# Moving the return of x ahead of the powers' row, the loads and the stores in SyncE's queue of a gated linear attention and cosine MLP kernel

## The chip, the cores and the metric

The kernel runs on one core of one Trainium2 chip. The metric is the device time of one execution in microseconds (us), as the median of several runs. The profile is of one further execution, whose own time is given beside its span (from its first to its last recorded instruction).

## What is computed

An attention-like recurrence, then an MLP with a cosine gate. Cut to what matters:

```python
# q, k, v, a_re, a_im: (B, H, S, D) = (4, 8, 768, 48)
mag = sqrt(a_re**2 + a_im**2)
scale = minimum(mag, 0.999) / (mag + 1e-6)
ar, ai = a_re * scale, a_im * scale              # a complex decay per step and channel
for t in range(S):
    S_re, S_im = ar*S_re - ai*S_im + k[t] (x) v[t], ar*S_im + ai*S_re
    y[t] = q[t] @ S_re
x = y.transpose(0, 2, 1, 3).reshape(3072, 384)
h = x @ w_in                                     # 384 -> 2048
out = (h * cos(h)) @ w_out                       # 2048 -> 384
```

## The kernel before, in words

The sequence is cut into 24 chunks of 128 steps, six to a batch. Two chunks make a group g, of which there are 12 (0 to 11). A group passes through these steps, and each step of it is a function of `fast_path`:

- `load`: re, im, k, q, v of the group come from memory by DMAs on SyncE's queue.
- `log_steps` (`logs`): the logarithm of the decay's size and the tangent of its half angle. ScalarE squares re and im (`lg<-re`, `tan<-im`), loads a table, takes `lg`, `mag`, `rs`; VectorE does `lg<-lg,tan`, `mag<-re,mag`, `lg<-lg`, `lg<-lg,rs`, `mag<-mag,tan`, `lo<-lg,hi`, `tan<-...`, in turn with ScalarE.
- `p_powers`, `g_carry`, `g_split`, `even_steps`, `p_apply` (`prods`): TensorE sums the logarithms along the chunk (`lgs`), ScalarE exponentiates them into P (kept in the buffer of `lg`) and Q, VectorE rounds them and multiplies k and q by them (`Q<-k,Q`, `mag<-q,lg`).
- `row_out`, `row_back`: the last row of P goes to memory as `row` (one packet of 3072 bytes) and comes back transposed as `end` (96 partitions x 16 elements; two DMAs of 768 elements of 4 bytes each). `p_end` halves `end` and keeps its least value. `state_next` reads `end`.
- `g_phase`, `g_trig`, `g_stack` (`phases`, `keys`): the angles are summed (`phs`), their sine and cosine taken, and `ks` and `qs` formed. `f_transpose` turns them by way of memory: a block transpose on VectorE (`tr`), a DMA to memory (`moved`), and DMAs back as `kT` (four) and `qT` (one). All of these are on SyncE's queue.
- `chunks`: for each chunk two `f_scores` (TensorE's `sc`, masked by VectorE into the halves of `atm`: four heads each), `f_state` (`sp`, then `state` on VectorE), and `f_out` (`yp`: eight heads in pairs, each atm half read by two pairs; where a chunk has a state, its product with q is added). ScalarE copies `yp` into `yT`. After the group's second chunk `f_x` writes yT to memory as `x` (two DMAs), and `f_xt` reads it back, laid out for the MLP, as `xT`.
- `mm1_sums`, `gate_sine`, `gate_product` (`first`): `hp` = w_in times xT on TensorE, in eight parts of 12 matmuls; ScalarE takes the cosine (`gate`) and a square sum (`junk`), VectorE the product.
- `mixed`, `seventh` (`mixes`, `products`): from group 2 on the second product is done by a seven-product scheme. VectorE forms sums and differences of gates (`s`); TensorE's `sum` and `op` accumulate; ScalarE and VectorE write `ot`; a store on SyncE's queue writes it out. Groups 0 and 1 use `mm2`, with its own store.

The main loop runs over n from 2 to 11. An iteration begins with the scores of group n, and beside them stand the logs of group n+1 and the second product of group n-1; then come the keys of n+1 and, from 0.56 of the iteration on, the first product of group n. `weave` sets the order in which the instructions are written down, by the fractions beside each part. In TensorE's queue this order is binding, since `matmul` chains each instruction to the one before. On VectorE, ScalarE and SyncE the order in this loop is left to the scheduler, which places instructions by its own estimate of when they can run; `behind(a, b)` keeps a behind b in a queue, without a wait of its own.

Every vector and scalar operation is recorded at the helper's lines L676 (`Ordered`) and L707 (`special`), and matmuls at L687, so they are told apart by their tiles. The DMAs concerned are recorded at these lines: L581 and L584 loads, L835 `row`, L842 `end`, L933 `moved`, L936 `kT`, L938 `qT`, L1048 `x`, L1057 `xT`, L1113, L1196 and L1202 stores.

In SyncE's queue of a steady iteration the order is: re and im of group n+2 (ten DMAs), `row`, `x` twice, `end` twice, `k`, `xT`, `k`, `q` twice, `v` twice, two stores, `moved` twice, `kT` four times, `qT`.

Of the kernel before, what the change touches and what calls it, by code (L numbers as in the profile page):

```python
# [487 lines left out]
def fast_path(ctx, tc, q, k, v, a_re, a_im, moe_w_in, moe_w_out, out, least, odd, wide,  # L488
# [7 lines left out]
    nc = tc.nc  # L496
    B, H, S, D = q.shape
    DM, DF = moe_w_in.shape
    C = 128
    NCH = S // C  # L500
    G = 2
    N = B * NCH
    NG = N // G
# [30 lines left out]
    late = {}  # L534
# [8 lines left out]
    def behind(ins, other):  # L543
        tc.add_manual_dep(ins.ins, other.ins.name, mybir.DependencyInfo(
            mybir.DependencyClass.NoSync, mybir.DependencyReason.DATA))
# [14 lines left out]
    X = [dict() for _ in range(NG)]  # L560
# [6 lines left out]
    def load(g, names, i=None, put=nc.sync.dma_start):  # L567
        for name in names:
            ap = {"re": a_re, "im": a_im, "q": q, "k": k, "v": v}[name]
            if name not in X[g]:  # L570
                X[g][name] = ld.tile([C, G, H, D], F32, tag=name, name=name,
                                     bufs=2 if name == "v" else 1)
            b, c = divmod(g * G + (i or 0), NCH)
            one, n = i or 0, G if i is None else 1
            steps = ap[b].rearrange("h (c p) d -> p c h d", p=C)[:, ds(c, n)]
            tile_ = X[g][name][:, ds(one, n)]
            parts = [(0, C, 0)]
            if name in ("re", "im") and g >= PEG:

                parts = [(0, C - 16, 1), (C - 16, C - 1, 1)]  # L580
                put(out=tile_[C - 1:C], in_=steps[0:1])  # L581
            for i_ in range(n):
                for lo, hi, by in parts:
                    put(out=tile_[lo:hi, i_], in_=steps[lo + by:hi + by, i_])  # L584
# [227 lines left out]
    def even_steps(g, i, n):  # L812


        x = X[g]
        u = cut(x["mag"], i, n)
        P, Q = cut(x["P"], i, n), cut(x["Q"], i, n)
        ins = [vector.scalar_tensor_tensor(out=u, in0=Q, scalar=HUGE, in1=P,
                                           op0=ALU.min, op1=ALU.mult)]
        yield  # L820
        for t in P, Q:
            ins.append(vector.scalar_tensor_tensor(out=t, in0=u, scalar=3.0, in1=t,
                                                   op0=ALU.subtract, op1=ALU.mult))
            yield

        for one_, what in zip(ins, ("carried", "split")):
            if what in x and g > PEG:
                behind(one_, x[what])
        if g > 0:
            row_out(g, i, n, nc.sync)  # L830
            row_back(g, i, n, nc.sync)

    def row_out(g, i, n, queue):
        P = cut(X[g]["P"], i, n)
        queue.dma_start(out=X[g]["row"][ds(i * DM, n * DM)],  # L835
                        in_=P[C - 1:C].rearrange("o x -> (o x)"))

    def row_back(g, i, n, queue):
        row = X[g]["row"][ds(i * DM, n * DM)]
        end = X[g]["end"][:, ds(i * H, n * H)]  # L840
        for a in range(2):
            queue.dma_start(out=end[ds(a * D, D)], in_=row.rearrange("(x d) -> d x", d=D))  # L842
# [209 lines left out]
    def f_xt(g, i=0, n=G):  # L1052

        if i == 0:
            X[g]["xT"] = msb.tile([C, ND, G, C], F32, tag="xT", name="xT")
        moved = X[g]["moved"].rearrange("p s d g t -> (p s d) g t").rearrange("(c r) g t -> r c g t", r=C)
        put = nc.sync.dma_start(out=X[g]["xT"][:, :, ds(i, n)], in_=moved[:, :, ds(i, n)])  # L1057
        behind(put, late["x"])
        late["x"] = put

    def mm1_sums(g, jp, i=None):

# [39 lines left out]
    def mm2(g, i, j0, nj):  # L1102
        if j0 == 0:
            Y[g * G + i]["op"] = pm.tile([C, DM], F32, tag="acc" if g == i else "m", name="op",
                                         bufs=1 if g == i else 2)
        ps = Y[g * G + i]["op"]
        for j in range(j0, j0 + nj):
            matmul(ps, lhsT=X[g]["gate"][j // 2][:, j % 2, ts(i, C)], rhs=w_out[:, j],
                   start=(j == 0), stop=(j == NJ - 1))
        if j0 + nj == NJ:  # L1110
            ot = msb.tile([C, DM], F32, tag="ot", name="ot")
            scalar.mul(out=ot, in_=ps, mul=1.0 / (in_scale * out_scale))
            nc.sync.dma_start(out=out[ts(g * G + i, C), :], in_=ot)  # L1113

# [1 line left out]
    PLAIN, HJ, E2 = 2, NJ // 2, DM // 2  # L1118
# [41 lines left out]
    def seventh(g, p, part):  # L1160


        x, name = X[g], SEVEN[p]
        if p == 0 and part == 0:
            x["sum"] = pm.tile([C, E2], F32, tag="acc", name="sum", bufs=1)
            x["ot"] = [msb.tile([C, DM], F32, tag="ot", name="ot") for _ in range(G)]

        alone = g == NG - 1 and p == 6
        summed = p in (0, 3, 5, 6) and not alone
        if not summed and part == 0:  # L1170
            x["op"] = pm.tile([C, E2], F32, tag="m", name="op", bufs=2)
        ps = x["sum"] if summed else x["op"]
        for j in range(part * HJ // 2, (part + 1) * HJ // 2):
            matmul(ps, lhsT=left(g, name, j), rhs=right[name][:, j],
                   start=(j == 0 and (p == 0 or not summed)),
                   stop=(j == HJ - 1), skip_group_check=summed)
        if part == 0:
            return
        c11, c12, c21, c22 = (x["ot"][i][:, ts(half, E2)] for i in range(2) for half in range(2))
        if g == NG - 1:  # L1180
            c12 = rest
        if p in (0, 3, 5) or p == 6 and not alone:
            late["scalar"] = scalar.mul(out={0: c11, 3: c21, 5: c22, 6: c12}[p], in_=ps, mul=scale)
        if g == NG - 1 and p == 5:
            scalar.mul(out=c12, in_=ps, mul=scale)
        for part_ in {1: [c11], 2: [c21], 4: [c21, c22], 6: [c12] * alone}.get(p, []):
            added = vector.scalar_tensor_tensor(out=part_, in0=ps, scalar=scale,
                                                in1=part_, op0=ALU.mult, op1=ALU.add)
            if alone:
                behind(added, late["read DVE"])  # L1190
            late["vector"] = added
        row = g * G * C
        if g == NG - 1 and p == 1:
            behind(nc.sync.dma_start(out=out[ds(row, C), 0:E2], in_=c11), late["line"])
        elif p == 4:
            put = nc.sync.dma_start(out=out[ds(row + C, C), :], in_=x["ot"][1])  # L1196
            if g == NG - 1:
                behind(put, late["read SP"])
        elif p == 6 and alone:
            late["store"] = lambda: nc.scalar.dma_start(out=out[ds(row, C), E2:DM], in_=c12)  # L1200
        elif p == 6:
            nc.sync.dma_start(out=out[ds(row, C), :], in_=x["ot"][0])  # L1202
# [40 lines left out]
    def prods(g):  # L1243
        if not 0 <= g < NG:
            return
        if g not in (1, 2):
            yield from powers(g)
            yield lambda: g_angle(g, 0, G)
        yield lambda: (g_carry(g), g_split(g))
        yield lambda: (p_even(g, 0, G), p_apply(g, 0, G))  # L1250
# [9 lines left out]
    def chunks(g):  # L1260
        for n in range(g * G, g * G + G):
            for hh in range(2):
                yield lambda n=n, hh=hh: f_scores(n, hh)
            yield lambda n=n: f_state(n)
            yield lambda n=n: f_out(n)
        yield lambda: (f_x(g), f_xt(g))
        if g + 2 < NG:
            yield lambda: load(g + 2, ("k", "q", "v"))

    def first(g):  # L1270
        order = range(NJ // 2) if g < PLAIN else (0, 4, 1, 5, 2, 6, 3, 7)
# [2 lines left out]
    def second(g, i):  # L1274
        return [lambda j0=j0: mm2(g, i, j0, 4) for j0 in range(0, NJ, 4)] if g < PLAIN else []
# [292 lines left out]
    for n in range(2, NG):  # L1568
        weave((mixes(n - 1, 2, 4), 0.0, 0.12), (logs(n + 1), 0.0, 0.02), (chunks(n), 0.0, 0.36),
              (upper[2:] if n == 2 else [], 0.0, 0.2), (products(n - 1, 0, 2 + (n < NG - 1)), 0.0, 0.36),  # L1570
              (prods(n + 1), 0.25, 0.27), (second(n - 1, 1), 0.36, 0.5),
              (products(n - 1, 2 + (n < NG - 1), 7), 0.4, 0.56),
              (phases(n + 1), *((0.472, 0.476) if n == PLAIN else (0.516, 0.524))),
              (keys(n + 1), *((0.5, 0.62) if n == PLAIN else (0.53, 0.64))),
              (last_quarter() if n == PLAIN else [], 0.9, 1.0), (first(n), 0.56, 1.0),
              (mixes(n, 0, 2), 0.9, 1.0), (guarded(n - 1, per) if n > 3 else [], 0.1, 0.9))
# [101 lines left out]
```

## Time and profile before

| what | value |
|---|---|
| time, median of 3 runs | 655.01 us (654.78 to 655.53) |
| the profiled execution's own time | 653.01 us |
| its span | 651.2 us |
| granted TensorE clock | 1.0 throughout |
| first matmul of the eight hp parts of groups 2 to 11 | at 153.8, 204.2, 255.4, 305.6, 355.9, 407.1, 457.4, 507.7, 559.4, 607.5 us |
| first score matmul of n=3 to 11 | at 174.6, 224.9, 276.1, 326.3, 376.7, 427.9, 478.1, 528.5, 580.1 us |
| DMA | 94.90 MB, 146 GB/s on average |
| DMA packets under 512 B | 208701 of 232920 |

How to read it: times in a timeline are from the span's start, in us. A row of a timeline has start, duration, engine, line, operation, tiles written and read, shape and count; in square brackets stands idle time of the engine before it and what ended it. PE is TensorE's matmul side, PEld its weight loads, DVE VectorE, ACT ScalarE, POOL GpSimd, SPq the queue of SyncE, which issues DMAs; the duration of such a row is that of the issue. A DMA's landing is read from the updates of its semaphore in the trace.

### The profile page before, as it was taken

What the parts mean: (1) busy time and instruction counts of PE and PEld (TensorE: products, weight loads), DVE (VectorE), ACT (ScalarE), POOL (GpSimd) and SP (SyncE); (2) the same over time, 40 slices, a digit from 0 to 9 for tenths busy, and PEclk for the clock granted to TensorE, in tenths of its full rate; (3) what the DMA queues carried; (4) which work ended last, traced back from release to release, by engine and by line L of the source; (5) the groups of instructions that cost most, each with busy time, mean ns of one, the idle gap of its engine ahead of it and who ended that gap; (6) DMA issues with size and microseconds to landing.
All of it is one profiled execution on the core that took longest, in us unless ns stands there. A gap on an engine that the chain in (4) does not pass through costs nothing.

```text
span 651.2 us, 10758 instructions
## 1 busy us (share of the span) xinstructions
PE 641.0 (98%) x4075; PEld 576.4 (89%) x4075; DVE 492.0 (76%) x799; ACT 392.8 (60%) x726; POOL 30.9 (5%) x53
## 2 busy tenths in 40 slices
PE   8999999999999999999999999999999999999997
PEld 6888877777999999899899899899899999999996
DVE  6999989888687688786787787876877878862251
ACT  7898687284583593494494485485576476433330
POOL 4010200000000000010010010000000000000000
PEclk9999999999999999999999999999999999999999
DMA  9968755727627656747738737836836843363001
GB/s 249 244 179 203 225 164 123 170 62 182 146 49 182 158 146 148 194 110 167 209 82 191 204 85 167 205 96 151 226 105 146 219 123 98 112 134 120 25 1 31
DMA packets 232920, 94.90 MB, mean 146 GB/s; under 512 B 208701, under 2 KB 221246, under 8 KB 232858
## 3 DMA queue, kind: packets, MB, share of 16 engines
q1 hardware_dynamic: 225320, 68.51, 45.3%
q0 software_dynamic: 5824, 25.50, 11.7%
q8 instruction: 34, 0.56, 0.4%
q10 hardware_dynamic: 1714, 0.11, 0.2%
q14 instruction: 28, 0.23, 0.1%
HBM read 69.28 MB, written 24.81 MB: 144 GB/s over the span
## 4 chain that ended last, share of the span: by engine, by line
PE 92%; ACT 4%; DVE 3%; DMA 0%; issue 0%; SPq 0%; DVEq 0%
PE hp L687 38%; PE op L687 18%; PE sum L687 16%; PE sc L687 6%; PE yp L687 6%; PE sp L687 4%; PE phs L687 2%; PE lgs L687 1%; ACT tan L707 1%; PE yr L687 1%; PE tp L948 1%; ACT rs L707 1%; ACT lg L707 1%; ACT L703 1%; DVE mag L676 1%; DVE atm L676 1%
## 5 line engine op out<-in xcount | busy, mean ns | idle before, releaser
L687 PE MATMUL hp<-xT,w_in 128*128 128x256 f32 (+1 forms) x1176 | 252.5, 375 | 0.0
L687 PEld LDWEIGHTS hp<-xT,w_in 128*128 128x128 f32 x1176 | 219.6, 190 | 30.2 <-issue 0.2
L707 ACT ACTIVATE gate<-hp,half_pi_b 128x512 f32<-128x512 f32 x96 | 66.0, 687 | 118.5 <-PE hp L687 118.5
L687 PE MATMUL op<-w_out,gate 128*128 128x192 f32 (+1 forms) x448 | 100.7, 374 | 0.0
L676 DVE TENSOR_TENSOR gate<-hp,gate 128x512 f32<-128x512 f32 x96 | 65.7, 684 | 45.8 <-ACT junk L676 45.7
L687 PEld LDWEIGHTS op<-w_out,gate 128*128 128x128 f32 x448 | 75.9, 190 | 16.9 <-issue 2.0
L676 ACT ACTIVATE junk<-hp 128x512 bf16<-128x512 f32 x96 | 56.7, 591 | 0.0
L687 PE MATMUL sum<-t_s,s 128*128 128x192 f32 x320 | 56.3, 329 | 0.0
L687 PEld LDWEIGHTS sum<-t_s,s 128*128 128x128 f32 x320 | 52.1, 190 | 1.5 <-issue 1.5
L676 DVE TENSOR_TENSOR atm<-sc,causal 128x512 f32<-128x512 f32 x48 | 32.9, 689 | 23.4 <-PE sc L687 23.4
L687 PEld LDWEIGHTS sc<-qT,kT 96*128 96x128 f32 x384 | 47.4, 192 | 2.3 <-issue 0.6
L687 PE MATMUL sc<-qT,kT 96*128 96x128 f32 x384 | 49.0, 276 | 0.2 <-ACT qT L676 0.2
L676 ACT ACTIVATE ot<-sum 128x192 f32<-128x192 f32 x39 | 12.6, 322 | 53.7 <-PE sum L687 53.4
L676 DVE SCALAR_TENSOR_TENSOR ot<-op,ot 128x192 f32<-128x192 f32 x40 | 13.3, 354 | 38.0 <-PE op L687 36.4
L687 PE MATMUL yp<-atm,v 128*48 128x128 f32 x352 | 33.6, 277 | 0.9 <-ACT Q L707 0.6
L703 ACT ACT_TABLE_LOAD x24 | 30.8, 1283 | 1.2 <-PEq L1662 0.7
L676 ACT COPY yT<-yp 48x512 f32<-48x512 f32 x44 | 25.3, 574 | 7.4 <-PE yp L687 7.0
L687 PE MATMUL yp<-qT,state 96*48 96x128 f32 x304 | 29.7, 272 | 0.0
L687 PE MATMUL sum<-w_out,gate 128*128 128x192 f32 x160 | 29.7, 329 | 0.0
L687 PE MATMUL sp<-v,ks 128*96 128x48 f32 x320 | 29.7, 245 | 0.0
L687 PEld LDWEIGHTS sp<-v,ks 128*96 128x96 f32 x320 | 29.6, 165 | 0.0
L676 ACT CAST tan<-phs 128x384 int32<-128x384 f32 x24 | 11.4, 480 | 29.4 <-PE phs L687 29.4
(147 smaller groups left out, 987.4 us busy)
## 6 DMA issues: line engine op xcount, KB each, us to landing
moved<-tr SPq DMA_DIRECT2D x20, 768.0 KB
raw<-in_moe_w_in_dram POOLq DMA_DIRECT2D x16, 768.0 KB, 5.1
raw<-in_moe_w_out_dram POOLq DMA_DIRECT2D x16, 768.0 KB, 4.6
kT<-moved SPq DMA_DIRECT2D x40, 192.0 KB
qT<-moved SPq DMA_DIRECT2D x10, 768.0 KB
k<-in_k_dram SPq DMA_DIRECT2D x24, 192.0 KB
q<-in_q_dram SPq DMA_DIRECT2D x24, 192.0 KB
v<-in_v_dram SPq DMA_DIRECT2D x24, 192.0 KB
```

Of the source, the lines that this page charges most:

```text
L676: ins = getattr(self.engine, op)(**kw)
L687: chain(nc.tensor.matmul(out, **kw), "tensor")
L703: chain(nc.scalar.preload_act_table_set(table))
L707: chain(nc.scalar.activation(func=func, **kw))
L948: chain(nc.tensor.transpose(ps[:, h], X[g][name[0] + "s"][:, x0 + h].rearrange("p a d -> p (a d)"), ident), "tensor")
```

## The change

`row_out` and `row_back` no longer stand at the end of `even_steps` for the groups of the main loop, but in a function `ends`, which the main loop calls at 0.36 of the iteration, behind `xT` of the group before. The loads of k, q and v of group n+2 are kept behind that `xT` too, and so are the stores of the group before it: the second store of `mm2` and that of `seventh`'s product 4. The groups 0 to 2 write and read their rows where they did.

```diff
@@ even_steps
-        if g > 0:
-            row_out(g, i, n, nc.sync)
-            row_back(g, i, n, nc.sync)
+        if 0 < g <= PLAIN:
+            ends(g)
+
+    def ends(g):
+        put = row_out(g, 0, G, nc.sync)
+        if g > PLAIN:
+            behind(put, X[g - 1]["back"])
+        row_back(g, 0, G, nc.sync)
 
     def row_out(g, i, n, queue):
         P = cut(X[g]["P"], i, n)
-        queue.dma_start(out=X[g]["row"][ds(i * DM, n * DM)],
-                        in_=P[C - 1:C].rearrange("o x -> (o x)"))
+        return queue.dma_start(out=X[g]["row"][ds(i * DM, n * DM)],
+                               in_=P[C - 1:C].rearrange("o x -> (o x)"))
@@ f_xt
         behind(put, late["x"])
-        late["x"] = put
+        late["x"] = X[g]["back"] = put
@@ mm2
-            nc.sync.dma_start(out=out[ts(g * G + i, C), :], in_=ot)
+            put = nc.sync.dma_start(out=out[ts(g * G + i, C), :], in_=ot)
+            if g > 0 and i > 0:
+                behind(put, X[g + 1]["back"])
@@ seventh
-            if g == NG - 1:
-                behind(put, late["read SP"])
+            behind(put, late["read SP"] if g == NG - 1 else X[g + 1]["back"])
@@ chunks
-            yield lambda: load(g + 2, ("k", "q", "v"))
+            yield lambda: load(g + 2, ("k", "q", "v"), put=lambda **kw: behind(
+                nc.sync.dma_start(**kw), X[g]["back"]))
@@ main loop
-              (prods(n + 1), 0.25, 0.27), (second(n - 1, 1), 0.36, 0.5),
+              (prods(n + 1), 0.25, 0.27),
+              ([lambda: ends(n + 1)] if n + 1 < NG else [], 0.36, 0.37), (second(n - 1, 1), 0.36, 0.5),
```

In the built program SyncE's queue of a steady iteration then runs: re and im of group n+2, `x` twice, `xT`, `k` twice, `q` twice, `v` twice, `row`, two stores, `moved` of ks, `end` twice, `moved` of qs, `kT` four times, `qT`.

## The prediction, as it was put on record

> **What bounds the kernel now.** I read the page's busy times and chain first, then the waits by engine, then the timeline of one steady iteration, engine by engine.
>
> ```profile
> PE 641.0 (98%) x4075; PEld 576.4 (89%) x4075; DVE 492.0 (76%) x799; ACT 392.8 (60%) x726; POOL 30.9 (5%) x53
> ...
> PE 92%; ACT 4%; DVE 3%; DMA 0%; issue 0%; SPq 0%; DVEq 0%
> ```
>
> TensorE is the bound, and it has almost no idle time: in the table of stretches it is busy 12.00 of 12.00 us from 142 to 154, 30.00 of 30.00 from 175 to 205, and so on to 647. A share of busy time can hide slow matmuls, so I also read the distance from one matmul start to the next: 216 ns for all hp of 256 columns, 163 ns for all sum and op of 192. From 142 us on I find only three real waits, the first `lgs<-lo` at 288.4, 440.2 and 540.9, of 0.40, 0.40 and 0.35 us. So there is about 1.15 us to be won after the start, and any new wait of TensorE is paid in full.
>
> The change acts on SyncE's queue. This is its timeline in the iteration n=3 (start us, us, engine, line, what):
>
> ```profile
> 190.00 2.85 SPq L584 DMA_DIRECT2D im<-in_a_im_dram  x4
> 196.10 0.24 SPq L835 DMA_DIRECT2D row<-lg  x1
> 196.43 0.81 SPq L1048 DMA_DIRECT2D x<-yT  x2
> 197.35 1.30 SPq L842 DMA_DIRECT2D end<-row  x2
> ...
> 199.59 0.45 SPq L1057 DMA_DIRECT2D xT<-x  x1
> ```
>
> yT was complete on ScalarE at 192.74, but `x` stands behind `row`, which waits for VectorE's `lg` (ends 196.03). `xT` lands at 203.38 (the trace's landing events) and the hp that reads it start at 204.16, without a gap. In the other groups the margin is 0.4 to 1.4 us.
>
> The place that decides is the start of an iteration. Below, TensorE's yp of n=4 (its first score matmul starts at S = 224.88), then VectorE, then ScalarE:
>
> ```profile
> 230.75 0.43 PE L687 MATMUL yp<-atm,v 128*48 128x128 f32 x4
> ...
> 231.67 0.39 PE L687 MATMUL yp<-atm,v 128*48 128x128 f32 x4
> ```
> ```profile
> 227.84 0.96 DVE L676 TENSOR_TENSOR lg<-lg,tan 128x768 f32<-128x768 f32 x1
> 228.72 0.68 DVE L676 TENSOR_TENSOR atm<-sc,causal 128x512 f32<-128x512 f32 x1
> ...
> 230.97 0.96 DVE L676 SCALAR_TENSOR_TENSOR mag<-re,mag 128x768 f32<-128x768 f32 x1
> 231.85 0.56 DVE L676 TENSOR_SCALAR lg<-lg 128x768 f32<-128x768 f32 x1
> ```
> ```profile
> 226.15 0.20 ACT L676 ACTIVATION_READ_ACCUMULATOR junk<-hp 128x1 f32 x1
> ...
> 230.10 0.84 ACT L707 ACTIVATE mag<-lg 128x768 f32<-128x768 f32 x1
> 230.85 0.83 ACT L707 ACTIVATE rs<-lg 128x768 f32<-128x768 f32 x1
> ```
>
> The yp of heads 0 to 3 (from 230.75) read the first masked half, atm1; those of heads 4 to 7 (from 231.67) read the second, atm2, which was done at 229.40. `mag<-re` starts 0.03 us after ScalarE's `mag` ends (230.94): it is bound by ScalarE. That chain (squares, table load, lg, mag) begins when the last junk of the group before ends, so it is tied to TensorE's hp and cannot come sooner.
>
> [...] in these stretches no record of VectorE overtakes another. [...] the 1024-byte packets of `xT`, issued behind both `end`, begin at about 200.7, when their 4-byte packets are through (200.5).
>
> **The change, part by part.** Its own lines only move SyncE's work, but the built order of all engines shows more. TensorE's order is the same to the instruction (it is chained by hand). VectorE's and ScalarE's are set by a scheduler, and there the sequence changes from the iteration n=4 on:
>
> ```
> n            VectorE from the last two gates on
> before 4-10  atm1 gate s lg+ atm2 s gate s state mag lg ...
> after 4,6,9  gate s s lg+ gate atm1 s mag lg atm2 ...
> after 7,10   gate s s lg+ atm1 gate s mag lg atm2 ...
> after 5,8    gate s s lg+ atm1 gate s atm2 (state) mag lg ...
> ```
> (lg+ is `lg<-lg,tan`, mag `mag<-re,mag`, lg `lg<-lg`; in n=6 and 9 state follows later.) n=3 and n=11 keep the old order here.
>
> 1. *x, xT ahead of row.* x can be issued at 192.9 (after im's issue) instead of 196.43, so xT lands about 3.5 us sooner. Its reader does not wait today: gain 0. Cover: the sum matmuls until 204.16.
> 2. *k, q, v behind xT.* They wait for the last readers of their buffers, `Q<-k,Q` (ends 196.90) and `mag<-q,lg` (197.77), and are issued up to 1.8 us sooner; their readers come some 45 us later. While SyncE waits there, `row`, the stores and `moved` are queued behind; none of them is wanted before the first transpose ends at 209.55, some 5 us after the last load is issued (204.9 today). 0.
> 3. *row behind the loads, end between the two moved.* `row` (one packet) is issued near 203 and is there before `end`, which now follows `moved<-tr` of ks (issued 209.57) while SyncE waits for the second transpose (ends 212.37). The issues of `end` (1.30 us) fit in. Their 1536 packets of 4 bytes took about 1.3 us of data; they fall into a hole of some 1 us between the two moved and push the train moved, kT, qT back by perhaps 0.3 us. qT lands ahead of its first score by 1.14, 0.55, 0.98, 0.48, 0.76, 0.97, 0.13, 1.09 us in n=4 to 11. At 0.3 only n=10 waits: 0.2 us. Bounds: 0, and at 1.4 us (nothing fits the hole) 5.1 us in all.
> 4. *p_end later on VectorE* (0.17+0.14 us, behind the third or fourth gate). moved's packets are through at about 212.4, so `end` lands near 214.5 (1.3 us of data and 0.7 us until the landing shows, as for moved: 212.76); its place comes near 215.1, where the third gate ends today. If it were late, the gates behind it wait; the hp buffers have about 2 us of slack. 0. The stores keep their place: 0.
> 5. *atm2 behind mag and lg.* VectorE in n=4, as times after S: the last gate can start when junk ends (1.47), then s, s, lg+ (3.03), gate, atm1 (4.24 to 4.93), s. `mag` still waits for ScalarE: 6.09. Behind it in the queue stand lg and atm2, and TensorE waits for atm2. Then lg at +0.88, 6.97, atm2 at +0.47, 7.44, and 0.69 long: 8.13. A matmul follows the end of atm by 0.06 (seen at 141.29 to 141.35). TensorE needs it at 6.79 (231.67 - 224.88): it waits 8.19 - 6.79 = **1.39 us**. n=7 ends alike. In n=6 and 9 no state is added, the yp take half as long and atm2 is wanted at 6.34: **1.84 us**. In n=10 the ot that stood ahead of ScalarE's mag moves away, so all is 0.2 sooner: **1.20 us**.
> 6. *n=5 and 8.* atm2 is in time (5.86). ScalarE's `ot<-sum` (0.21) moves behind `hi`, and atm3 behind `lo` and `tan`. So `lo` ends at 287.85, and the wait of 0.40 at 288.4 is gone; but atm3 now ends at 289.33 and atm4 at 290.80, where the yp want them at 289.16 and, after the first wait, 290.27. They end at 291.74 instead of 291.46: **+0.28** each. In the other iterations the later TensorE covers this; n=10's wait of 0.35 disappears.
>
> Sum: 2 x 1.39 + 2 x 1.84 + 1.20 - 0.35 + 2 x 0.28 + 0.2 = 8.1 us. No idle time of TensorE follows that could take it up. The profiled execution is 653.01 (span 651.2 and 1.8 around it), so 661.1 for one like it. The median of the timed runs, 655.01, is 2.0 longer; I keep that distance: **663.1 us**.
>
> **Rivals.** *A, not slower: atm2 isn't held.* Place: `mag<-re` on VectorE. If it started by S+4.7 (6.79 - 0.06 - 0.69 - 1.35), atm2 would be in time. Then only the three lgs waits count, 655.01 - 1.15 = 653.9; and if the timed runs are 2.0 longer because xT is late there (margins from 0.4 us), up to 2 us more. Against it: ScalarE's chain stands the same in seven iterations, mag ending at S+6.06. *B, more: the train behind end is late.* Place: qT in the eight iterations; it decides once the push passes 0.5 us. At 1.4 us: 655.01 + 7.9 + 5.1 = 668.0. For it: small packets and margins below 1 us; against it: the hole between the two moved. That SyncE's order isn't as announced is ruled out by the built order.
>
> **Numbers.** Mine 0.79, with its own range 660.5 to 666 (0.3 us either way on five stalls, qT from 0 to 2 us); A 0.12; B 0.09. The range 659 to 667.5 takes in part of B and leaves A out. A measurement of this kernel can tell about 0.2% (1.3 us). A splits evenly: faster 0.06, same 0.06; mine and B are slower: 0.88.
>
> **What would show it.** Right: TensorE waits for `DVE atm` of 1.2 to 1.9 us in n=4, 6, 7, 9 and 10 and none in n=3 and 11; `mag<-re` ahead of atm2, still S+6.1; the lgs waits gone; xT landing 4 us or more ahead of hp. Wrong: `mag<-re` well before S+6 (A), or scores waiting for qT (B), or hp waiting at a group's start for any reason.

## The result, and the profile after

| | before | after |
|---|---|---|
| time, median of 4 runs each | 655.27 us (654.78 to 655.72) | 662.15 us (661.78 to 663.64) |
| ratio, with its 95% interval | | 1.0112 [1.0088, 1.0135] |
| own time of the profiled execution | 653.01 us | 662.21 us |
| its span | 651.2 us | 660.4 us |
| last matmul | 646.21 us | 654.83 us |

Slower by 1.1%: the change costs 6.9 us between the medians, and 9.2 us between the two profiled executions. That these differ by 2.3 us is a result of its own, taken up below.

The page after, engines and chain of waits. TensorE is 1.0 us busier in a span 9.2 us longer, and the chain runs more often over the other engines (ScalarE 4% to 11%):

```profile
PE 642.0 (97%) x4075; PEld 575.5 (87%) x4075; DVE 492.5 (75%) x799; ACT 393.7 (60%) x726; POOL 31.4 (5%) x53
...
PE 82%; ACT 11%; DVE 4%; issue 1%; DMA 0%; ACTq 0%; SPq 0%; DVEq 0%
```

The waits of TensorE after (us in total, times, longest), the two that answer to the change. Waits for `atm` now lead the list (0.3 us, once, in the profile before; of the 8.6 some 0.9 lie at 140 to 141 us, in n=2, where TensorE starts no later than before). No hp waits for xT, and the qT row is short:

```profile
PE yp L687 <- DVE atm L676: 8.6, 11, 1.7
...
PE sc L687 <- DMA qT<-moved: 0.2, 1, 0.2
```

SyncE's queue after, in the same iteration n=3. `x` is issued at 193.27 instead of 196.43 and `xT` at 196.46 instead of 199.59; it lands at 199.86, 4.3 us ahead of the first hp (before: 0.8). The issue of `end` (1.75 us) fits between the two `moved`:

```profile
193.27 0.82 SPq L1053 DMA_DIRECT2D x<-yT  x2
196.46 0.38 SPq L1062 DMA_DIRECT2D xT<-x  x1
...
202.19 0.44 SPq L840 DMA_DIRECT2D row<-lg  x1
...
209.50 0.33 SPq L938 DMA_DIRECT2D moved<-tr  x1
209.91 1.75 SPq L847 DMA_DIRECT2D end<-row  x2
212.23 0.34 SPq L938 DMA_DIRECT2D moved<-tr  x1
```

So SyncE's queue does what the change says, and the transfer that it hurries is 4.0 to 5.7 us early in the groups 3 to 10, where before it had 0.4 to 1.5 in seven of these eight. The time is lost at the start of the iteration. TensorE, VectorE and ScalarE in n=4 after, in one view by start (S = 224.87):

```profile
229.10 0.69 DVE L676 TENSOR_TENSOR atm<-sc,causal 128x512 f32<-128x512 f32 x1
...
230.08 0.84 ACT L707 ACTIVATE mag<-lg 128x768 f32<-128x768 f32 x1
...
230.96 0.96 DVE L676 SCALAR_TENSOR_TENSOR mag<-re,mag 128x768 f32<-128x768 f32 x1 [0.84 <-ACT mag L707]
...
231.44 0.39 PE L687 MATMUL yp<-qT,state 96*48 96x128 f32 x4
...
231.83 0.55 DVE L676 TENSOR_SCALAR lg<-lg 128x768 f32<-128x768 f32 x1
232.30 0.69 DVE L676 TENSOR_TENSOR atm<-sc,causal 128x512 f32<-128x512 f32 x1
...
233.04 0.43 PE L687 MATMUL yp<-atm,v 128*48 128x128 f32 x4 [1.22 <-DVE atm L676]
```

VectorE stands idle for 0.84 us until ScalarE's `mag` is done, with atm2 behind `mag<-re` and `lg<-lg` in its queue. The scores that atm2 masks had been ready since 228.1 (the end of the second run of `sc`). TensorE, which began these yp at 231.67 before, begins them at 233.04. `mag<-re` starts at S+6.09, to 0.01 us where it started before.

All waits of TensorE that differ between the two first profiles, read from the starts of matmuls (how much later a matmul begins than before; the idle time in square brackets of a timeline comes out up to 0.17 us shorter, since the ends of matmuls in a trace are modelled):

| place | forecast | measured |
|---|---|---|
| atm2, n=4 and 7 | 1.39 each | 1.38, 1.39 |
| atm2, n=6 and 9 | 1.84 each | 1.83, 1.83 |
| atm2, n=10 | 1.20 | 0.99 |
| atm3 and atm4 less the lgs wait, n=5 and 8 | 0.28 each | 0.39, 0.63 |
| lgs wait of n=10 gone | -0.35 | -0.35 |
| qT | 0.2 | 0.15 (n=5) + 0.38 (n=10) |
| sum | 8.1 | 8.6 |

The last matmul moved by 8.62 us, so nothing else on TensorE changed; the remaining 0.58 us of the span lies behind the last matmul (5.60 us to the end instead of 5.02).

### The profile page after: what moved, and what is told of

Its sections match the earlier page's. It is cut to its first block, busy times and chain, and to the rows that moved or that the text cites. A ratio compares the mean times of both kernels' runs of the same rounds, so it can differ in the third digit from the quotient of the medians.

```text
span 660.4 us, 10792 instructions
## 1 busy us (share of the span) xinstructions
PE 642.0 (97%) x4075; PEld 575.5 (87%) x4075; DVE 492.5 (75%) x799; ACT 393.7 (60%) x726; POOL 31.4 (5%) x53
## 4 chain that ended last, share of the span: by engine, by line
PE 82%; ACT 11%; DVE 4%; issue 1%; DMA 0%; ACTq 0%; SPq 0%; DVEq 0%
PE hp L687 37%; PE op L687 17%; PE sum L687 13%; PE yp L687 4%; PE sc L687 4%; PE sp L687 2%; PE phs L687 2%; ACT L703 2%; ACT lg L707 2%; ACT tan L707 1%; ACT mag L707 1%; DVE mag L676 1%; ACT rs L707 1%; DVE tan L676 1%; PE lgs L687 1%
## 5 line engine op out<-in xcount | busy, mean ns | idle before, releaser
L687 PEld LDWEIGHTS yp<-atm,v 128*48 128x48 f32 x352 | 19.0, 122 | 15.3 <-DVE atm L676 9.9
```

The lines of the kernel that those rows point to most:

```text
L687: chain(nc.tensor.matmul(out, **kw), "tensor")
```

## Experiments

Theory 1: VectorE's order is what the change costs; SyncE's new order by itself costs only some qT and saves the waits for xT. Theory 2: SyncE's new queue costs the time, through something that lands late (the forecast's rival B is one form of it), and VectorE only shows it.

**hold: VectorE's atm2 put back, SyncE's new queue kept.**

```diff
-        vector.scalar_tensor_tensor(out=mag, in0=re, scalar=0.0, in1=mag,
-                                    op0=ALU.max, op1=ALU.add)
+        wide_ = vector.scalar_tensor_tensor(out=mag, in0=re, scalar=0.0, in1=mag,
+                                            op0=ALU.max, op1=ALU.add)
+        if g > 3:
+            behind(wide_, Y[(g - 1) * G]["masked"])
```
(The steps of `log_steps` from there on are written down after atm2, which `behind` needs.)

> The changed kernel with mag<-re kept behind atm2 on VectorE in n=4 to 10; SyncE's queue keeps its new order to the instruction. Theory 1 (VectorE's order costs the time: atm2 behind mag<-re and lg<-lg): the five stalls of 1.38, 1.83, 1.39, 1.83 and 0.99 us go, 7.4 in all, and part comes back at atm4, which still stands behind lo and tan: in n=6 and 9 it ends about S+14.85 where TensorE wants it at S+14.41, so 0.44 each. Time 662.15 - 7.4 + 0.9 = 655.6 us, no wait of TensorE for atm in a first chunk. Theory 2 (SyncE's new queue costs it, by whatever came late through it): within 1 us of 662.15.

Measured: 656.34 us, ratio to before 1.0015 [1.0002, 1.0028]. Of the 6.9 us nearly 6 are gone with SyncE's queue unchanged to the instruction. Its waits of TensorE:

```profile
PE yp L687 <- DVE atm L676: 2.7, 8, 0.6
...
PE sc L687 <- DMA qT<-moved: 0.5, 1, 0.5
```

No first chunk waits in n=4 to 10. What is left sits in the second chunk, as expected there: 0.44 and 0.42 at atm4 in n=6 and 9, 0.88 and 0.96 for atm3 and atm4 in n=5 and 8 (0.40 of each replaces the lgs wait). 0.67 at qT in n=10 and 0.26 for `ot` in n=6 were not expected. Theory 2 is refuted: it wanted 662.

**order_only: the kernel before with VectorE's bad order.**

```diff
+        x["capped"] = vector.tensor_scalar(out=m2, ...)
...
+        if hh == 1 and n % G == 0 and n // G in (4, 6, 7, 9, 10):
+            behind(y["masked"], X[n // G + 1]["capped"])
```

> The kernel before with atm2 kept behind lg<-lg on VectorE in n=4, 6, 7, 9 and 10; SyncE's queue as before. Theory 1: stalls of 1.39 (n=4, 7), 1.84 (n=6, 9) and 1.77 (n=10, where mag<-re comes at S+6.46 here), less the lgs wait of n=10 (0.35): 7.9 us, so an own time of the profiled execution near 660.9, and 663.2 us timed if the timed runs of before stay 2 us above its profile; 661 if that distance belongs to SyncE's old order and is hidden by the later TensorE. Theory 2: 655.3 us.

Measured: 663.29 us, ratio 1.0122 [1.0105, 1.0139], as much as the whole change costs, with SyncE's queue as before to the instruction. Its waits of TensorE for atm:

```profile
PE yp L687 <- DVE atm L676: 7.6, 6, 1.7
```

The stalls are 1.38, 1.83, 1.38, 1.83 and 1.74 us. In these five iterations the scheduler also moved some later operations of VectorE (`atm3`, `atm4`, `raw<-raw`, the two of `p_end`), but no wait of TensorE shows at them. Necessary (hold) and sufficient (order_only): the cause is shown. Its own profiled execution took 665.21, 4.3 more than expected; 3.3 of that is a lower clock (0.50) behind two of the stalls, shown at the end.

**no_row and only_row: one half of the change each.** no_row keeps `row` and `end` where they were and moves the loads and stores behind xT:

```diff
-        if 0 < g <= PLAIN:
+        if g > 0:
             ends(g)
...
-              ([lambda: ends(n + 1)] if n + 1 < NG else [], 0.36, 0.37), (second(n - 1, 1), 0.36, 0.5),
+              (second(n - 1, 1), 0.36, 0.5),
```

> Only the k, q, v loads and the stores behind xT; row and end where they were, so x stays behind row. VectorE has atm1 and atm2 ahead of mag<-re in every iteration, but atm3 and atm4 behind lo and tan. Theory 1: no wait in a first chunk; atm4 late by about 0.39 to 0.52 us in n=5, 6, 8 and 9, 1.8 in all, the lgs waits of 1.15 gone: 655.3 + 1.8 - 1.15 = 655.9 us. A theory that the loads and stores behind xT cost the time gives 660 or more.

only_row moves `row` and `end`, and drops the three edits that put loads and stores behind xT:

> Only row and end moved behind xT; loads of k, q, v and the stores not kept behind it (two loads of k go ahead of xT). VectorE has atm1 and atm2 ahead of mag<-re everywhere; atm3 and atm4 behind lo and tan in n=5 and 8. Theory 1: no wait in a first chunk; n=5 and 8 cost 0.39 and 0.52, the lgs wait of n=10 goes, qT 0.5: an own time near 653.6 and 653.6 to 655.8 timed. If moving row is by itself what costs the time: 660 or more.

Measured: 658.74 us (1.0058 [1.0043, 1.0073]) and 659.35 us (1.0054 [1.0037, 1.0071]). In neither does a first chunk wait: each half alone leaves atm1 and atm2 ahead of `mag<-re`, and only both together bring the bad order about. Both came out slower than expected, for other reasons. In no_row xT is issued behind `end` still and hp waits for it by 0.75, 0.29 and 0.51 us in groups 4, 6 and 7 (with 0.6 for `ot` and 0.4 for qT beside it):

```profile
PE hp L687 <- DMA xT<-x: 0.9, 2, 0.6
```

In only_row one iteration (n=2) has the second `moved` behind the four kT (issued at 166.69 instead of 161.93), qT lands at 176.57, and the scores of n=3 wait 2.2 us, and the matmuls behind them run at a lower clock (0.55 from 176.8 to 178.5 us and 0.50 to 180.4; last section). The other expected waits were there (0.37 and 0.46 in n=5, 0.57 and 0.46 in n=8, less the lgs).

**hold2: atm3 put back as well; a store got ahead of xT.** `mag<-mag,tan` is kept behind atm3, by the same kind of edit. SyncE's queue is the changed one but for one store.

> The changed kernel with both orders of VectorE given back: mag<-re behind atm2, and mag<-mag,tan behind atm3, in n=4 to 10. SyncE keeps its new order but for one store, which goes ahead of xT. Theory 1: no wait for atm at all, the lgs waits of about 0.4 us in n=5, 8 and 10 come back, qT costs 0.5 us: 655.3 + 0.5 = 655.8 us timed if an earlier xT gives nothing, down to 653.5 us if the timed runs of before lose 2 us to a late xT. Theory 2: near 662.

Measured: 703.38 us, 1.0745 [1.0727, 1.0764]. VectorE's order is right everywhere, and both theories missed, by 48 and 41 us. Its SyncE and TensorE near the start of the hp of group 3:

```profile
193.32 0.82 SPq L1059 DMA_DIRECT2D x<-yT  x2
204.91 0.36 SPq L1214 DMA_DIRECT2D out_dram<-ot  x1
205.37 0.38 SPq L1068 DMA_DIRECT2D xT<-x  x1
...
208.96 0.77 PE L687 MATMUL hp<-xT,w_in 128*128 128x256 f32 x1 [4.50 <-DMA xT<-x]
```

The store waits for an `ot` that is written late (its issue comes at 204.91), and xT behind it leaves 8.9 us later than in the changed kernel. In seven groups hp waits 4.5 to 4.8 us, and the matmuls behind run at a lower clock (0.50 from 209 to 212 us behind the first of these waits; last section), which takes most of another 2.2 to 3.0. One instruction that waits, one place too early in a queue: 48 us. The store is that of product 6, which the change does not tie to xT: in the changed kernel it stands behind xT only because the scheduler put it there. hold2_store, hold3 and hold4 below tie it.

**hold2_store, hold3, hold4: can VectorE be set right without a new wait?** All three keep both stores behind xT, so SyncE's queue is the changed kernel's, and hold atm2 as above. hold2_store keeps `mag<-mag,tan` behind atm3, hold3 keeps `tan<-mag,tan` behind atm4, hold4 keeps `tan<-tan,im` behind atm4:

```diff
+            behind(wide_, Y[(g - 1) * G + 1]["masked"])
...
-            nc.sync.dma_start(out=out[ds(row, C), :], in_=x["ot"][0])
+            behind(nc.sync.dma_start(out=out[ds(row, C), :], in_=x["ot"][0]), X[g + 1]["back"])
```

> The changed kernel with mag<-re behind atm2 and mag<-mag,tan behind atm3 and both stores behind xT, so SyncE's queue is that of the changed kernel to the instruction. On VectorE lo comes ahead of atm3 from n=5 on, and atm4 ahead of tan<-mag. Theory 1 (VectorE's order is what costs; SyncE's queue costs only qT): no wait for atm, no lgs wait from n=5 on (1.15 us gone), qT 0.3 to 1 us; an own time of 653.0 - 1.15 + 0.7 + 0.6 of tail = 653.2; timed 653.2 if xT was the 2 us of before, 655.0 if not. That the store ahead of xT was what took 48 us in the run with the store ahead: this one has no hp waiting for xT. Theory 2 (SyncE's queue costs it): 660 or more.

> The changed kernel with mag<-re behind atm2 and tan<-mag behind atm4 on VectorE, and both stores behind xT; SyncE's queue is the changed kernel's. VectorE then runs mag<-mag,tan, lo, atm3, atm4, tan. From the trace of the changed kernel: mag<-mag,tan from about S+10.3, so lo ends near S+12.1, atm3 near 12.7, atm4 near 13.4, where TensorE wants them at S+12.3, 13.0 and 13.9 at the earliest. Theory 1 (VectorE's order is what the change cost; SyncE's new queue by itself gains the xT waits of before): no wait for atm in n=4 to 10, no lgs wait, qT up to 1 us, xT none: own and timed time 653 to 654, 2 to 3 us under before. If SyncE's new queue has a price beside VectorE's order, it is 658 or more.

> The changed kernel with mag<-re behind atm2, tan<-tan,im behind atm4, and both stores behind xT. VectorE: mag<-mag,tan, lo, tan, atm3, atm4, tan<-tan,im. Against the run that only held mag<-re, atm4 ends 0.9 us sooner, about S+14.1 where TensorE wants it at S+14.4, and atm3 stays where it was (0.02 to 0.1 us late in n=5 and 8 beyond the lgs wait that it replaces). If that is all: 656.3 - 1.8 = 654.5 us. If raw<-raw on VectorE, which waits for a weight load, holds ScalarE's hi and ot behind it again, as it did in the run that held tan (2.5 us in n=6), it is 657 or more.

Measured: 659.24 (1.0055 [1.0038, 1.0071]), 658.91 (1.0050 [1.0037, 1.0064]) and 658.73 us (1.0052 [1.0035, 1.0069]). What theory 1 says of atm holds in each: first chunks wait nowhere, and in hold3 no atm and no lgs wait is left from n=3 on. But the gain went into new waits. In hold2_store `lo` now waits for ScalarE's `hi` with atm3 behind it, and the lgs wait doubles to 0.78 in n=5 and 8:

```profile
288.66 0.96 DVE L676 SCALAR_TENSOR_TENSOR lo<-lg,hi 128x768 fp32r<-128x768 f32 x1 [2.44 <-ACT hi L728]
289.53 0.68 DVE L676 TENSOR_TENSOR atm<-sc,causal 128x512 f32<-128x512 f32 x1
```

In hold3 it is a weight load. `raw<-raw` on VectorE waits for it, `tan<-tan,carry` stands behind, ScalarE's `hi` waits for that, `ot<-sum` stands behind, and TensorE waits for `ot`. Its VectorE, ScalarE and TensorE in n=6:

```profile
348.80 0.56 DVE L676 TENSOR_SCALAR raw<-raw 128x768 uint32<-128x768 uint32 x1 [4.88 <-DMA raw<-in_moe_w_in_dram]
349.39 0.62 DVE L676 SCALAR_TENSOR_TENSOR tan<-tan,carry 32x384 f32<-32x384 f32 x1
```
```profile
350.04 0.84 ACT L728 ACTIVATE hi<-tan 128x768 fp32r<-128x768 f32 x1 [3.85 <-DVE tan L676]
350.91 0.33 ACT L676 ACTIVATE ot<-sum 128x192 f32<-128x192 f32 x1
```
```profile
351.29 0.92 PE L687 MATMUL sum<-t_s,s 128*128 128x192 f32 x4 [2.36 <-ACT ot L676]
```

hold4 has the same chain in n=6 (5.13 us of VectorE before `raw<-raw`, 2.8 of TensorE for `ot`). In hold, hold2_store, hold3 and hold4 this weight load of n=6 is issued alike, 13.5 us after S, but VectorE has it at S+18.98, 19.94, 20.78 and 21.02; why it comes later was not found. The expectation of hold3 named 658 us or more as the sign that SyncE's new queue has a price of its own, and hold3 (658.91) came out there. The waits are for `ot` and qT, but whether the new queue has a part in the late load stays open. In hold, with the same queue, no more than about 1 us is left to explain. No version found is faster than before; hold, within 0.3% of it, is the nearest.

**hold2_store_end and end_first: `end` ahead of the first `moved`**, once on hold2_store (with `lo` kept ahead of `mag<-mag,tan`), once on the changed kernel alone.

```diff
+        if name == "kT":
+            behind(put, X[g]["returned"])
```

> As the run before it, with end also ahead of the first moved, and lo ahead of mag<-mag,tan. Theory 1: the 4-byte packets of end are gone before moved's, so qT no longer waits: 0.5 us less than the run before it, 652.7 or, if xT wasn't the 2 us, 654.5. If end, which waits for row to land, holds the first moved, the scores wait for qT by up to 1 us in each iteration and it is slower than the run before it by up to 8 us.

> The changed kernel with end ahead of the first moved instead of between the two; atm2 stays behind mag<-re and lg<-lg in n=4, 6, 7, 9 and 10. Tests the price of end between the two moved (0.2 us in the forecast, bounds 0 and 5.1), which shows only as qT coming late for the scores of n=5 and 10 (0.53 and 1.51 us in the two profiles of the changed kernel). Theory 1: the five stalls for atm2 stay as they are, qT waits 0 to 1.0 us: 661.2 to 662.2 us. Theory 2 (the train behind end is the larger part of the cost): under 659.

Measured: 678.32 us (1.0346 [1.0330, 1.0362]) and 663.50 us (1.0131 [1.0111, 1.0151]). In end_first the five stalls for atm2 are 1.38, 1.83, 1.39, 1.83 and 1.03, and qT waits only once (0.36 in n=10). So `end` between the two `moved` is worth at most about 1 us, and taking it out gained nothing: the scores of n=3 begin 0.6 us later, which this execution lost at the start of the kernel, ahead of all that the edit touches (the `lgs` at 9.8 and 12.3 us wait for VectorE), and 0.43 is lost to atm4 in n=3. hold2_store_end was wrong about its mechanism: qT waits 0.9 in all, but the scheduler put `raw<-raw` ahead of atm2, and atm2 waits with it for a weight load:

```profile
284.77 0.56 DVE L676 TENSOR_SCALAR raw<-raw 128x768 uint32<-128x768 uint32 x1 [2.51 <-DMA raw<-in_moe_w_in_dram]
285.24 0.68 DVE L676 TENSOR_TENSOR atm<-sc,causal 128x512 f32<-128x512 f32 x1
```

**before_again and after_again: a second profile of each kernel**, to settle the 2.3 us.

> The kernel before, for a second profile: its profile of the forecast (653.01 us) lies 2.2 us under its timed median (655.24). If the distance is xT landing behind its first hp in most executions, hp waits here for xT by some 2 us in all at the starts of groups, and the own time is near 655. If it is the granted clock or the stretch around the span, no such wait is seen at an own time near 655.

> The changed kernel, for a second profile. If the stalls for atm are set by the order of VectorE and ScalarE, they come back at the same places with the same sizes to 0.05 us (1.38, 1.83, 1.39, 1.83, 0.99), no hp waits for xT, and only the waits for qT differ from run to run.

Measured: 656.37 and 662.24 us. Before has waits in this execution that its first profile lacks, one hp for xT in group 8 (matmul starts 1.69 us late) and the scores of n=10 for qT (0.84 late):

```profile
PE hp L687 <- DMA xT<-x: 1.5, 1, 1.5
...
PE sc L687 <- DMA qT<-moved: 0.7, 1, 0.7
```

Where the late xT comes from stands 11 us earlier on VectorE of the same execution:

```profile
448.28 0.56 DVE L676 TENSOR_SCALAR raw<-raw 128x768 uint32<-128x768 uint32 x1 [3.18 <-DMA raw<-in_moe_w_out_dram]
...
450.49 0.95 DVE L676 SCALAR_TENSOR_TENSOR lg<-mag,lg 128x768 f32<-128x768 f32 x1
```

In the first profile that wait was 1.36 us and `raw<-raw` began at 446.36. Here the weight load, issued at the same place (441.29 for 441.18), is 1.8 us later, so `lg` is, so `row` is issued at 451.50 instead of 449.61, and `x` and `xT` behind it; xT lands at 459.03, where in the first profile hp had begun at 457.4. Why it took longer was not found. That `x` stands behind `row` is the dependency that the change cuts, and in both profiles of the changed kernel no hp waits.

after_again has the stalls of n=4, 6 and 9 again to 0.01 us (1.38, 1.83, 1.83), but n=7 has 1.17 and n=10 0.41. In n=10 the scores had waited 0.96 for qT in this execution, and 0.38 in the first: qT and atm2 make 1.37 together in both. The expectation was wrong there: `mag<-re` is tied to the hp before, not to the scores, so what TensorE loses to qT it does not lose again to atm2. The same holds for n=7: its scores began 0.21 us late behind the last hp, and the stall for atm2 is 0.22 shorter.

## Why the prediction was right

It said 663.1 us and slower; the median was 662.15, in its range. The mechanism was the right one; that the number came out within 1 us was in part luck, as the point on the distance from profile to median shows.

- **Step 5, atm2 behind mag and lg, right.** 7.42 us of the forecast 7.66; the two experiments hold and order_only show it as the cause, from both sides. Only n=10 was mis-sized, 0.99 for 1.20, by two slips: `mag<-re` came no sooner than in n=4 (the forecast took off 0.2 for the `ot` that moves away), and 0.38 of the delay went to qT instead, which with atm2 makes 1.37.
- **Step 6, n=5 and 8, right in kind, too small.** 0.39 and 0.63 for 0.28 each. A part is a slip in its sum: with atm4 done at 290.80 and 0.06 us to the matmul, the yp begin at 290.86, and in the profile before they began at 290.48; that is 0.38. The rest is n=8, where atm3 put the yp 0.57 us after their place (0.33 in n=5; reckoned 0.23).
- **Steps 1 and 2, right for the profile they were made from.** xT came early, and TensorE gained nothing against that profile. (Its margins for xT, 0.4 to 1.4 us, leave out groups 10 and 11, where xT was over 4 us early already.)
- **Step 3, the term was too small.** qT cost 0.53 us in one profile for 0.2, and 1.7 in the other (0.55, 0.21 and 0.96 in n=5, 7 and 10), of which the parts in n=7 and 10 came off the stalls for atm2. But before_again shows 0.84 of qT without the change, so not all of it is the price of `end`.
- **Step 4, right.** No wait for `end` shows on TensorE.
- **The distance from profile to median, wrong.** 2.0 us were kept on top of the profiled sum. The first profile of before was a fortunate execution, without the xT and qT waits of before_again (653.01 us against 656.37); the changed kernel's two profiles (662.21 and 662.24) lie on its median. Against the profile the sum was 1.1 us too small (steps 3 and 6 and 0.58 behind the last matmul, less 0.2 in n=10), and the 2.0 were too much by 2.1. The two errors cancelled to 0.95, which was luck; without it 661.1 would have stood in the range as well.
- **Rival A** guessed at the second half of this, that timed runs could lose up to 2 us to a late xT. That gain is real as far as before_again shows it, 1.7 us in one execution; the stalls for atm2 alone are four times that. **Rival B** fell: in the changed kernel qT never cost more than about 1 us in one place.

What the title of the change names, SyncE's queue, takes away a wait for xT that one of two profiles of before has (1.7 us), and brings waits for qT (0.5 to 1.7 us); that it gains anything in all is not shown, as no version with it was faster than before. The loss came from a side effect. VectorE's order in this loop is the scheduler's, made from its own estimate; with the DMAs moved it put a ready operation behind one that waits. no_row and only_row show that neither half of the edit does that alone. Why the scheduler chose so was not looked into.

## What to carry to other kernels

Where a scheduler sets the order of the engines' queues, compare the built order of every engine before and after an edit, not the diff: an edit of one queue can reorder another, and the price is read from the place in the queue where an operation that is ready now stands behind one that waits (here atm2, its scores ready at 228.1, ran at 232.30, behind a `mag<-re` that began at 230.96). Each such stall is priced well by hand (arrival of what is waited for, plus the operations between, less the moment of need), but setting it right by one constraint at a time only passes the wait on, as hold2, hold2_store, hold3 and hold4 did. One profile of a kernel with margins below 1 us is a sample: take a second before a difference of 2 us between profile and median is carried into a forecast.

## What the runs showed of the hardware that was not expected

In order_only the granted clock of TensorE fell to 0.50 behind an idle time of 1.7 us in n=6 (1.66 in the brackets of the timeline; the matmul begins 1.83 late). The stretches around it, the granted clock (PEclk) third from the end of each row, ahead of DMA share and GB/s:

```profile
334.00:336.30 2.30, 0.71 (x9) 0.39 (x8) 2.01 (x4) 2.30 (x5) 0.00 (x0) 1.00 0.55 226
336.30:337.20 0.90, 0.83 (x9) 0.65 (x10) 0.90 (x3) 0.90 (x2) 0.00 (x0) 0.94 0.00 0
337.20:339.60 2.40, 2.40 (x9) 2.40 (x9) 1.70 (x3) 2.39 (x6) 0.00 (x0) 0.50 0.05 10
339.60:342.00 2.40, 2.40 (x19) 2.40 (x18) 2.34 (x4) 1.61 (x3) 0.47 (x1) 0.81 0.79 154
```

The same place of the changed kernel, behind a stall of the same length:

```profile
337.30:339.60 2.30, 2.30 (x19) 2.30 (x19) 2.15 (x4) 2.30 (x6) 0.00 (x0) 1.00 0.05 10
```

19 matmuls there, 9 here; the eight op of 192 columns behind the stall take 2.62 us to the start of the next matmul, and 1.40 there (336.94 to 339.56, and 337.03 to 338.43). In order_only the yp of the second chunk come 1.65 us later after S than in the changed kernel, in n=6 and in n=9. From the rows above, 0.50 held in n=6 from about 337.1 to 340.5, 3.4 us (an estimate: what the rows on either side lack, 0.06 of 0.90 us and 0.19 of 2.40 us, is taken as time at 0.50). At half the clock that is 1.7 us of work, which fits the 1.65.

The clock was also lower behind idle times of 2.1 us (only_row, 0.55 and 0.50), 2.6 (hold4, 0.56 from 350.4 to 354.3 us), 1.9 to 2.6 (hold2_store_end, five times; mean clock of the execution 0.985) and 4.3 to 4.6 (hold2, all seven; 0.50 behind the first, mean 0.966). It was not behind 2.4 in hold3 (mean 0.998), nor behind the 1.7 of end_first (0.998) or of either profile of the changed kernel (0.998 and 1.0; what the first of these lacks lies at its end, 0.51 from 657.4 to 660.4, behind the last matmul). So the length of the idle time alone does not tell here whether the clock falls (1.66 us with a fall, 2.4 without); what else decides was not found. In order_only, where it did fall, a stall of 1.83 us cost 1.65 us more, nearly twice itself.
